# Two layernorm chunks as one background task: norms in two steps of three, scaling at the end

## The chip, the cores and the metric

The kernel runs on one core of one Trainium2 chip. The metric is the device time of one execution in microseconds (us); a kernel is judged by its fast executions (a slow one runs at a granted TensorE clock well below full speed). In the profile's lines PE is TensorE, the matmul engine, PEld its weight loads, DVE is VectorE, ACT ScalarE, POOL GpSimd and SP the engine that issues the transposing DMAs. Beside each time the profile gives the span, from the first to the last instruction; the time is 1.8 us longer than the span.

## The reference

One transformer block, 2048 rows of 1024, with a modulated layernorm ahead of both halves:

```python
h = _layernorm(x) * (1 + ca) + sa
x = x + ga * _A_ref(h, k_cache, v_cache, wq, wo)       # 32 heads over the last 512 keys, output projection
h = _layernorm(x) * (1 + cb) + sb
x = x + gb * _B_ref(h, w_gate, w_up, w_down)           # silu(h @ w_gate) * (h @ w_up) @ w_down, F = 3584
```

## The kernel before

The order is: attention of the first 1024 rows, their output projection, attention of the other 1024, their output projection, gate, up and down projection of the first half, then of the second. Large products are built from seven products of half size instead of eight; each of the seven passes over four row tiles of 128.

While such a projection runs, a background task prepares the layernorm of the next 1024 rows: two chunks of four row tiles. For a tile VectorE writes the normed rows to one of **two** row buffers, and a transposing DMA turns them into `hT`. Once a chunk's four tiles are turned, VectorE scales and shifts it in place. The task advances by one `yield` for each call of `run_bg`.

```python
def norm_turn(ch, tt, tiles, sl=None):
    t = ch * TPC + tt
    sl = t % 2 if sl is None else sl
    norm(t, t % 8, sl, half=True)                       # L438, VectorE, 0.54 us, writes row buffer sl
    T.op(Q_ln[sl], lambda: SP.dma_start_transpose(hT[ch % 2][:, :, tt * P:(tt + 1) * P], nscf[sl]),
         reads=[B_ns4[sl]], writes=[tiles[tt]])         # L465

def ln_task(ch, gi, ccol, cbuf):
    ...
    for tt in range(TPC):                               # TPC = 4
        norm_turn(ch, tt, tiles)
        yield
    for _ in range(3):
        yield
    for dt in range(DT):                                # DT = 8
        modulate(dst, bufs, dt, gi, ccol, cbuf, tiles)  # L443, VectorE, 0.41 us
        if dt % 2 == 1:
            yield
```

The host of the task is `seven_products`. `hook` loads weights and calls `run_bg(1)`; `out` is the residual pass, whose first instruction (L1117) reads the accumulator bank that a later product needs.

```python
for j in range(TPC):
    prod(0, j, AB[j], True, early[j])
    if own_s1:
        s1_sum(j)                                       # L1057, VectorE, 1.23 us
        s2_sum(j)                                       # L1041, VectorE, 1.23 us
    ...
    hook(0, j)                                          # steps 0 to 3; j == 3 first issues the load for product 2
for j in range(TPC):
    prod(1, j, BB_[j], True)
    out(0, j, 0, AB[j], BB_[j], None)                   # residual j frees bank AB[j]
    hook(1, j)                                          # steps 4 to 7
for j in range(TPC):
    prod(2, j, AB[j], False)                            # PE needs AB[j] again
    ...
```

The softmax here doesn't subtract the row's maximum and nothing guards it: scores larger than these inputs give would overflow.

Of the kernel before, what the change touches and what calls it, by code (L numbers as in the profile page):

```python
# [131 lines left out]
def bass_adaLN_cond__sliding_block_cached__swiglu_ffn__prompt_kernel(  # L132
# [14 lines left out]
    _, S, D = A_x.shape  # L147
# [6 lines left out]
    DT = D // P  # L154
# [5 lines left out]
    TPC = CH // P  # L160
# [58 lines left out]
    def bank(b, n=512, off=0):  # L219
        return ps[:, b * 512 + off:b * 512 + off + n]  # L220
# [14 lines left out]
    B_mode = _Buf("mode"); B_modc = _Buf("modc"); B_bq = _Buf("bq"); B_gf = _Buf("gf")  # L235
# [23 lines left out]
    with nc.Block() as block:  # L259

        @block.gpsimd
        def _(g):
# [5 lines left out]
            def mm(out_ap, lhsT, rhs, start, stop, reads, bank_buf, skip=False):  # L268
                T.op(PE, lambda: TE.matmul(out_ap, lhsT, rhs, start=start, stop=stop, skip_group_check=skip),  # L269
                     reads=reads, writes=[bank_buf])  # L270
# [5 lines left out]
            bg = []  # L276

            def run_bg(n=1):
                while n > 0 and bg:
                    try:  # L280
                        next(bg[0])
                        n -= 1
                    except StopIteration:
                        bg.pop(0)
# [88 lines left out]
            B_hT = [[_Buf("hT%d_%d" % (i, dt)) for dt in range(DT)] for i in range(2)]  # L373
            hT = [arena.at(OFF_H + i * 8 * KB, [DT, CH], F16, B_hT[i]) for i in range(2)]
# [61 lines left out]
            def norm(t, sl, ns, c0=0, n=D, half=False):  # L436
                o = (nscf if half else nsc4)[ns]
                T.op(DVE, lambda: V.tensor_scalar(o[:, c0:c0 + n], x_res[:, t, c0:c0 + n], mv[sl][:, 0:1], rstd[sl],  # L438
                                                  op0=ALU.subtract, op1=ALU.mult),
                     reads=[B_x[t], B_mv[sl], B_rs[sl]], writes=[B_ns4[ns]])  # L440

            def modulate(dst, bufs, dt, gi, ccol, cbuf, tiles):
                T.op(DVE, lambda: V.tensor_scalar(dst[:, dt, :], dst[:, dt, :], gain[gi][:, dt:dt + 1],  # L443
                                                  mod_bf[:, ccol + dt:ccol + dt + 1], op0=ALU.mult, op1=ALU.add),
                     reads=[B_g[gi], cbuf] + tiles, writes=[bufs[dt]])
# [8 lines left out]
            def ln_tiles(ch):  # L454
                tiles = [_Buf("hTt%d_%d" % (ch, tt)) for tt in range(TPC)]
                for tile in tiles:
                    for b_ in B_hT[ch % 2]:
                        tile.absorb(b_)
                return tiles
# [4 lines that stand above are left out]
                norm(t, t % 8, sl, half=True)  # L464
                T.op(Q_ln[sl], lambda: SP.dma_start_transpose(hT[ch % 2][:, :, tt * P:(tt + 1) * P], nscf[sl]),  # L465
                     reads=[B_ns4[sl]], writes=[tiles[tt]])

            def ln_task(ch, gi, ccol, cbuf):
                dst, bufs = hT[ch % 2], B_hT[ch % 2]
                tiles = ln_tiles(ch)  # L470
                for tt in range(TPC):
                    norm_turn(ch, tt, tiles)
                    yield
                for _ in range(3):
                    yield
                for dt in range(DT):
                    modulate(dst, bufs, dt, gi, ccol, cbuf, tiles)
                    if dt % 2 == 1:
                        yield

            def stats_task(t0, n):
                for t in range(t0, t0 + n):
                    yield from ln_stats(t)
# [859 lines left out]
            def o_phase(sc, hook):  # L1343
                load, ver = wo0[sc]
                n1 = _N1()
                sj = []

                def rings(tt, j, half):
                    if (tt, half) == (1, 0):
                        return sj[1 + j % 2]  # L1350
                    return tmp[j % 2][:, :], B_tmp[j % 2]

                def hk(idx, j):
                    if j == TPC - 1 and idx < 4:
                        load(idx + 2)
                    if idx == 4 and j == 0:
                        load(6)
                    if j == TPC - 1 and idx == 2:
                        for n in range(TPC):
                            b_ = _Buf("sj%d" % n)  # L1360
                            sj.append((arena.at((128 + 2 * n) * KB, [CH], F32, [b_]), b_))
                    hook(idx, j)

                seven_products(HP, oT, B_oT, OFF_OT, n1, ver, AB_O, BB_O, o_out(sc, sj, rings), sj, True, hk, (14, 14, 0, 0))
# [33 lines left out]

            while bg:
                run_bg(1)  # L1400
            for ch in (2, 3):
                bg.append(ln_task(ch, 0, 0, B_mode))
            o_phase(0, o_hook0)


# [30 lines left out]
            def w_slot(q):  # L1436
                return (q if q < FP else q + 2) % 3

            def take_w(q):
                p = q % FP  # L1440
                sl = w_slot(q)
                W_of[q] = [seven_at(OFF_W[sl] + 8 * KB * m, "w%d_%d" % (q, m), "own") for m in range(2)]
                for m, w in enumerate(W_of[q]):
                    src = (B_w_gate, B_w_up)[m][:, 256 * p:256 * p + 256].rearrange("(k q) n -> q k n", q=P)
                    T.op(Q_w[sl][m], lambda: SP.dma_start(w.raw, src), writes=[w.b_raw, w.b_s3])
# [15 lines left out]
            def ws(n):  # L1461
                for _ in range(n):
                    next(wsum[0], None)
# [18 lines left out]

            while bg:
                run_bg(1)
            for ch in (0, 1):
                bg.append(ln_task(ch, 1, 3 * DT, B_late[1]))
            o_phase(1, o_hook1)
            take_w(1)
            take_w(2)
# [149 lines left out]
            for sc in range(2):  # L1639
                q0 = sc * FP  # L1640

                def f_early(k0, k1):
                    for k in range(k0, k1):
                        va, vb = ver(0, k)
                        mm(bank(0), gu[0][:, k, 0:P], va, k == 0, False, [B_gu[0][k], vb], PB[0], skip=True)

                for r in range(FP + 1):
                    if sc == 0 and r == 2:
                        bg.append(stats_task(2 * TPC, 2 * TPC))
                    gate_up(q0 + r if r < FP else None, q0 + r - 1 if r > 0 else None, f_early if r == FP else None)  # L1650
                    run_bg(3)
                    if 1 <= r < FP - 2:
                        take_w(q0 + r + 2)
                    if r == FP - 2:
                        lq = q0 + FP - 1
                        d0, d1 = OFF_W[w_slot(lq - 2)], OFF_W[w_slot(lq - 1)]
                        load, ver = loader(sc, B_w_down, wd_sum, FP, "d", [[(o, FP)] for o in [d0, d1] * 3 + [d0]])
                        load(0)
                    if r == FP - 1:
                        load(1)  # L1660
                if sc == 0:
                    take_w(FP)
                b_sj = [_Buf("fj%d_%d" % (sc, j)) for j in range(TPC)]
                sj_t = arena.at(OFF_U, [TPC, CH], F32, b_sj)
                sj = [(sj_t[:, j, :], b_sj[j]) for j in range(TPC)]
                if sc == 0:
                    for ch in (2, 3):
                        bg.append(ln_task(ch, 1, 3 * DT, B_late[1]))

                def f_hook(idx, j):  # L1670
                    if j == TPC - 1 and idx < 5:
                        load(idx + 2)
                    run_bg(1)
                    if sc == 0 and idx == 6:
                        if j == 0:
                            while bg:
                                run_bg(1)
                            hs[0] = h_sums()
                            wsum[0] = w_sums(FP)
                        next(hs[0])  # L1680
                        ws(1)

                seven_products(FP, gu, B_gu, OFF_GU, m1, ver, (0, 1, 2, 3), (4, 5, 6, 7), f_out(sc), sj, False, f_hook, (10, 0, 0, 0), sc == 1)
                if sc == 0:
                    take_w(FP + 1)
                    take_w(FP + 2)
                    gu = [arena.at(OFF_GU[n], [FP, CH], F16, B_gu[n]) for n in range(4)]
# [31 lines left out]
```

## Time and profile before

| what | value |
|---|---|
| time, median of the 3 runs known at first | 1151.99 us (1151.91 to 1152.01) |
| span of the profiled execution | 1151.0 us (time of that execution 1152.78) |
| PE busy | 1138.7 us, 99% |
| VectorE (DVE) busy | 822.4 us, 71% |
| VectorE before a norm (L438), waiting for a transposing DMA | 24.8 us, 6 places, longest 7.3 |
| PE standing still behind L1117 | 1.15 us, once, at 570.64 us |

The lines are in the prediction. In a timeline or a chain the first number is the start, counted from the start of the span, the second the length; a bracket at the end gives the engine's idle time just before and what ended it. In a list of waits the numbers are the total, how often, and the longest.

### The profile page before, as it was taken

The page shows a single profiled execution, that of the slowest core. Times are in us where ns is not written, and L with a number is a line of the kernel's source. Part 1 is how long each engine was busy: PE and PEld are TensorE (multiplying, and loading weights), DVE is VectorE, ACT ScalarE, POOL GpSimd, SP SyncE. Part 2 cuts the span into 40 slices and gives each one's busy share as a digit, 9 for nine tenths or more (in the row PEclk, how much of TensorE's full clock was granted, in tenths as well). Part 3 has the DMA queues.
Part 4 walks back from the last instruction along what each step waited for, and adds up shares of the span by engine and source line. Part 5 has one row for each costly group of instructions (what it writes and reads, how often), then busy time and mean ns, then how long its engine had stood idle before and what let it go on. Part 6 is the DMA issues. An engine that isn't in the chain of part 4 may idle for free.

```text
span 1151.0 us, 17926 instructions
## 1 busy us (share of the span) xinstructions
PE 1138.7 (99%) x6906; PEld 584.3 (51%) x6991; DVE 822.4 (71%) x1644; ACT 525.6 (46%) x719; POOL 50.8 (4%) x107
## 2 busy tenths in 40 slices
PE   8999999999999999999999999999999999999999
PEld 5666665554446656656444444444444444444444
DVE  5768779857667777776667789877658777776536
ACT  4757777711137777777010354544110445444110
POOL 1100002100000000001000000000000000000000
PEclk9999999999999999999999999999999999999999
DMA  9889899987717998956784422323773433234343
GB/s 326 142 185 227 224 219 233 198 206 184 214 44 177 212 215 179 213 112 155 144 222 142 111 73 85 98 74 106 209 222 123 119 88 96 74 104 134 128 156 110
DMA packets 300373, 180.83 MB, mean 157 GB/s; under 512 B 140928, under 2 KB 289152, under 8 KB 300288
## 3 DMA queue, kind: packets, MB, share of 16 engines
q1 hardware_dynamic: 241632, 108.90, 41.9%
q10 hardware_dynamic: 54336, 55.05, 15.1%
q0 software_dynamic: 4320, 15.73, 4.7%
q8 instruction: 55, 0.90, 0.3%
q14 instruction: 30, 0.25, 0.1%
HBM read 126.75 MB, written 19.93 MB: 127 GB/s over the span
## 4 chain that ended last, share of the span: by engine, by line
PE 95%; DMA 2%; DVE 1%; issue 1%; ACT 1%; DVEq 0%
PE ps L269 95%; DMA arena<-nsc 1%; ACT arena L800 1%; DMA arena<-arena 0%; DVE st L424 0%; DMA x_res<-in_A_x_dram 0%; DVE arena L1057 0%; DVE nsc L438 0%; PE ps L273 0%; DVE arena L830 0%; DVE arena L847 0%; DVE arena L822 0%; DVE mv L544 0%; DVE arena L901 0%; DVE tmp L1117 0%
## 5 line engine op out<-in xcount | busy, mean ns | idle before, releaser
L269 PE MATMUL ps<-arena 128*128 128x512 f16 (+2 forms) x6693 | 1133.1, 330 | 9.0 <-POOL arena L416 2.0
L269 PEld LDWEIGHTS ps<-arena 128*128 128x128 bf16 (+1 forms) x6778 | 577.0, 98 | 559.3 <-DVE arena L830 4.5
L800 ACT ACTIVATE arena<-ps 128x1024 bf16<-128x1024 f32 x256 | 261.5, 1022 | 47.2 <-PE ps L269 35.4
L833 ACT ACTIVATE tmp<-ps 128x512 f32<-128x512 f32 x167 | 99.7, 597 | 299.8 <-PE ps L269 286.1
L901 DVE TENSOR_TENSOR arena<-arena 128x512 f16<-128x512 bf16 x328 | 133.3, 419 | 3.0
L830 DVE TENSOR_TENSOR arena<-ps,tmp 128x512 bf16<-128x512 f32 (+1 forms) x134 | 91.9, 686 | 52.2 <-PE ps L269 34.7
L833 ACT ACTIVATE nsc<-ps 128x512 f32<-128x512 f32 x84 | 50.1, 597 | 93.3 <-PE ps L269 90.9
L822 DVE TENSOR_TENSOR arena<-ps,rl 128x512 f16<-128x512 f32 x128 | 88.5, 691 | 4.7 <-DVE rl L819 0.2
L830 DVE TENSOR_TENSOR arena<-ps,nsc 128x512 f16<-128x512 f32 x84 | 57.3, 687 | 40.3 <-PE ps L269 30.0
L819 DVE RECIPROCAL rl<-ps 128x4 f32<-128x4 f32 x128 | 23.2, 181 | 74.8 <-PE ps L269 73.6
L1534 ACT ACTIVATE arena<-arena 128x512 f16<-128x512 f16 x84 | 49.8, 624 | 32.8 <-DVE arena L830 32.8
L1041 DVE TENSOR_TENSOR arena<-arena 128x2048 f16<-128x2048 f16 (+3 forms) x56 | 56.0, 1011 | 9.3 <-PE ps L269 8.8
L1117 DVE TENSOR_TENSOR tmp<-ps,tmp 128x512 f32<-128x512 f32 x32 | 22.1, 689 | 55.7 <-ACT tmp L833 46.1
L833 ACT ACTIVATE arena<-ps 128x512 f32<-128x512 f32 x16 | 9.6, 597 | 86.4 <-PE ps L269 86.4
L951 DVE TENSOR_TENSOR arena<-arena 128x512 f16<-128x512 bf16 x120 | 47.9, 420 | 1.0
L424 DVE BATCH_NORM_STATS2 st<-x_res 128x6 f32<-128x512 bf16 x58 | 39.6, 682 | 3.7 <-DMA x_res<-in_A_x_dram 3.4
L602 DVE SCALAR_TENSOR_TENSOR arena<-arena 128x1024 bf16<-128x1024 bf16 x32 | 38.9, 1216 | 0.0
L1549 DVE TENSOR_TENSOR arena<-arena 128x512 f16<-128x512 f16 x84 | 35.0, 417 | 0.3
L1118 DVE TENSOR_TENSOR tmp<-tmp,rowb 128x512 f32<-128x512 f32 (+1 forms) x49 | 33.6, 687 | 1.8
L438 DVE TENSOR_SCALAR nsc<-x_res,mv,rstd 128x1024 f16<-128x1024 bf16 (+1 forms) x30 | 16.2, 539 | 24.8 <-DMA arena<-nsc 24.8
L1119 DVE TENSOR_TENSOR arena<-tmp,x_res 128x512 bf16<-128x512 f32 (+1 forms) x33 | 22.3, 676 | 1.1
L830 DVE TENSOR_TENSOR arena<-ps,rowb 128x512 f16<-128x512 f32 x28 | 19.3, 689 | 3.8 <-ACT rowb L833 3.3
(80 smaller groups left out, 295.5 us busy)
## 6 DMA issues: line engine op xcount, KB each, us to landing
arena<-in_A_wq_dram SPq DMA_DIRECT2D x30, 512.0 KB, 5.2
arena<-wo_sum ACTq DMA_DIRECT2D x7, 2048.0 KB, 8.7
arena<-in_B_w_gate_dram SPq DMA_DIRECT2D x28, 512.0 KB, 3.9
arena<-in_B_w_up_dram SPq DMA_DIRECT2D x28, 512.0 KB, 5.1
arena<-wd_sum ACTq DMA_DIRECT2D x8, 1792.0 KB, 8.0
arena<-in_B_w_down_dram ACTq DMA_DIRECT2D x6, 1792.0 KB, 7.1
arena<-in_A_wo_dram POOLq DMA_DIRECT2D x16, 512.0 KB, 5.6
wo_sum<-arena SPq DMA_DIRECT2D x16, 512.0 KB, 4.0
```

What stands on the lines that cost most here:

```text
L269: T.op(PE, lambda: TE.matmul(out_ap, lhsT, rhs, start=start, stop=stop, skip_group_check=skip), reads=reads, writes=[bank_buf])
L424: T.op(DVE, lambda: V.bn_stats(st_[sl][:, hf * 6:hf * 6 + 6], x_res[:, t, hf * 512:hf * 512 + 512]), reads=[B_x[t]], writes=[B_st[sl]])
L602: T.op(DVE, lambda: V.scalar_tensor_tensor(mt[n % 2], mt[n % 2], 1.0, sc_row, op0=ALU.mult, op1=ALU.mult, accum_out=mcol[:, n:n + 1]), rea ...
L800: T.op(ACT, lambda: A.activation(ex_s[es][:, 2 * kp:2 * kp + 2, :], banks2(SCB + 2 * kp), AF.Exp, scale=att_scale), writes=[PB[SCB + 2 * k ...
L822: T.op(DVE, lambda: V.tensor_tensor(o_s[os_].rearrange("p (a b) d -> p a b d", a=2), psap(PVB * 512, [[512, 2], [130, 2], [1, P]]), rlb, A ...
L830: T.op(DVE, lambda: V.tensor_tensor(out, bank(ba), other, ADD), reads=[ob2], writes=[PB[ba], ob])
L833: T.op(ACT, lambda: A.activation(dst, bank(bk), AF.Copy), writes=[PB[bk], db])
L901: T.op(st, lambda: eng.tensor_tensor(o, a, b, op), reads=rd, writes=[wr])
L951: T.op(DVE, lambda: V.tensor_tensor(o, a, b, SUB), reads=rd, writes=[wr])
L1041: T.op(DVE, lambda: V.tensor_tensor(o, a, b, SUB), reads=rd, writes=[sb])
L1534: T.op(ACT, lambda: A.activation(o, s_, AF.Silu), reads=[sb], writes=[ob])
L1549: T.op(DVE, lambda: V.tensor_tensor(gu[blk][:, p, :], o, s_, MULT), reads=[sb, ob], writes=[B_gu[blk][p]])
```

## The change

The aim is that a norm no longer meets a row buffer that is still being transposed. The two chunks become one task; norms come in two steps of three; both chunks are scaled at the end.

```diff
-            def ln_task(ch, gi, ccol, cbuf):
-                dst, bufs = hT[ch % 2], B_hT[ch % 2]
-                tiles = ln_tiles(ch)
-                for tt in range(TPC):
-                    norm_turn(ch, tt, tiles)
+            def ln_pair(chs, gi, ccol, cbuf):
+                tiles = {ch: ln_tiles(ch) for ch in chs}
+                for n in range(2 * TPC):
+                    norm_turn(chs[n // TPC], n % TPC, tiles[chs[n // TPC]])
                     yield
-                for _ in range(3):
-                    yield
-                for dt in range(DT):
-                    modulate(dst, bufs, dt, gi, ccol, cbuf, tiles)
-                    if dt % 2 == 1:
+                    if n % 2 == 1:
                         yield
+                for ch in chs:
+                    for dt in range(DT):
+                        modulate(hT[ch % 2], B_hT[ch % 2], dt, gi, ccol, cbuf, tiles[ch])
+                        if dt % 2 == 1:
+                            yield
...
-            for ch in (0, 1):
-                bg.append(ln_task(ch, 1, 3 * DT, B_late[1]))
+            bg.append(ln_pair((0, 1), 1, 3 * DT, B_late[1]))
```

The same replacement is made in the first output projection and in the down projection.

More of the change, by code (lines that the diff above doesn't have):

```diff
@@ L1400, in _ @@
                 run_bg(1)
-            for ch in (2, 3):
-                bg.append(ln_task(ch, 0, 0, B_mode))
+            bg.append(ln_pair((2, 3), 0, 0, B_mode))
             o_phase(0, o_hook0)
@@ L1666, in _ @@
                 if sc == 0:
-                    for ch in (2, 3):
-                        bg.append(ln_task(ch, 1, 3 * DT, B_late[1]))
+                    bg.append(ln_pair((2, 3), 1, 3 * DT, B_late[1]))
                 def f_hook(idx, j):
```

## The prediction

> **What bounds the kernel now.** I read the page first, for the share of each engine; then the list of waits kept to the tensor engine; then the chain that ended last; then the timeline of the three stretches that the change touches, engine by engine.
>
> ```profile
> PE 1138.7 (99%) x6906; PEld 584.3 (51%) x6991; DVE 822.4 (71%) x1644; ACT 525.6 (46%) x719; POOL 50.8 (4%) x107
> ...
> DVE nsc L438 <- DMA arena<-nsc: 24.8, 6, 7.3
> ...
> PE ps L269 <- POOL arena L416: 2.0, 1, 2.0
> PE ps L269 <- DVE tmp L1117: 1.2, 1, 1.2
> PE ps L269 <- DVE arena L516: 0.5, 1, 0.5
> PE ps L269 <- DVE arena L830: 0.4, 2, 0.2
> PE ps L269 <- ACT arena L800: 0.3, 1, 0.3
> ```
>
> The first line says that PE is busy for 1138.7 of 1151.0 us: all that any change of order can give back is the 12.3 us in which it stands still. The second is the wait that the change is aimed at: VectorE stands for 24.8 us, in six places, before a norm of the layernorm (L438) because the row buffer that the norm writes is still being read by the transposing DMA of two tiles before. The last five are PE's own waits by releaser. Only one of them lies in a layernorm stretch and comes from VectorE's output code: 1.2 us, once, behind L1117, the first addition of a residual. So 24.8 us of VectorE's waiting show up as 1.2 us of PE's. The chain that ended last shows how the two hang together, in the output projection of the second half of the rows:
>
> ```profile
> 547.36 5.53 DMA arena<-arena
> 553.01 1.24 DVE arena L1057
> 554.31 1.10 issue
> 555.42 0.54 DVE nsc L438
> 555.99 10.50 DMA arena<-nsc
> 566.58 0.10 DVE nsc L438
> 566.68 0.36 issue
> 567.04 1.23 DVE arena L1057
> 568.33 1.11 issue
> 569.44 0.54 DVE nsc L438
> 569.98 0.61 DVE tmp L1117
> 570.64 27.80 PE ps L269 x128
> ```
>
> Columns are start, length, what. The chain leaves PE at 546 us, goes through VectorE and two transposing DMAs, and comes back to PE only at 570.64. The timeline of PE there has the gap itself (start, length, engine):
>
> ```profile
> 540.74 28.74 PE L269 MATMUL ps<-arena 128*128 128x512 bf16 x152
> 570.64 79.61 PE L269 MATMUL ps<-arena 128*128 128x512 f16 x366 [1.15 <-DVE tmp L1117]
> ```
>
> 540.74 + 28.74 = 569.48, then nothing until 570.64. What PE waits for at 570.64 is an accumulator bank: the third of the seven products adds into the banks of the first, and the first residual pass (L1117) has to read such a bank before PE may write it again.
>
> **What the Trainium skill says.** "Perfetto Trace Analysis", section "Optimization Strategy", says to find the gaps on the engine being optimised and what blocks it there. That is the reading used above; it leaves one gap in these stretches, not the 24.8 us. "PSUM — Partial Sum Buffer", section "Engine vs sequencer instructions": "ScalarE/VectorE/GpSimdE queues are strict FIFO." The trace agrees: the two sums of the fourth row tile, whose data were there when PE ended the first product at about 555.3, ran at 567.04 and 568.30, behind a norm that waited until 566.58. "DMA: Bandwidth & Descriptors", section "Issuing engines are not separate DMA queues", says that DMAs from different issuers end up on the same 16 engines and interleave. The trace agrees: the transposes issued at 555.99 and 558.84 from SP took 10.5 and 8.4 us, since ACT had issued a 2 MB load at 555.27 that landed at 564.64; the next two, with no load under way, took 3.06 us each. "TensorE: Matmul & The Clock Gate", section "Back-to-back issue gap", gives N/2.4 + 2.5 ns for an isolated matmul, 216 ns for N = 512; here ScalarE's evictions of successive products come 3.45 us apart (559.16, 562.62), 216 ns for each of the 16 matmuls, so PE is at its pace.
>
> **The change part by part.** I call one call of the hook after a row tile's product a step: 16 matmuls, 3.45 us, in the two output projections; 14, 3.02 us, in the down projection. Steps 0 to 3 belong to the first product, 4 to 7 to the second, and so on. Each step runs one piece of the background task, after that step's own VectorE work.
>
> Removed and added: no arithmetic. There are 8 norms at 0.54 us, 8 transposes and 16 scalings at 0.41 us per stretch in both. The old task has 22 steps: norms of chunk a in 0 to 3, empty 4 to 6, scaling in 7 to 10, norms of chunk b in 11 to 14, empty 15 to 17, scaling in 18 to 21. The new one has 20: norms in 0, 1, 3, 4, 6, 7, 9, 10, empty between, scaling of a in 12 to 15, of b in 16 to 19. Both end before step 23, where the sums over the transposed rows start, so no consumer comes forward. The direct saving of instructions is 0.
>
> Moved, in the stretch with the gap. Old order on VectorE: sums 0, norm 0, sums 1, norm 1, sums 2, norm 2 (waits until 566.58), sums 3, norm 3, residual. The residual can begin at 566.58 + 0.46 (norm issue) + 2.40 (two sums of 1.23, pipelined) + 0.46 (norm) = 569.90, which is what the timeline shows, and its bank is free at 569.90 + 0.68 = 570.58. New order: sums 0, norm 0, sums 1, norm 1, sums 2, sums 3, norm 2, residual 0, norm 3. Up to norm 1 (558.73) it is unchanged. Sums 2 and 3 take 4 x 1.23 and end by 563.7. Norm 2 waits for the same DMA, landed at 566.48, so it starts at 566.58 as before. The residual then starts at 566.58 + 0.46 = 567.04, 2.86 us earlier, and frees its bank at 567.72. PE arrives there at 569.48. So the whole 1.15 us goes, with 1.76 us to spare; the other 1.7 us of VectorE's gain are nothing to PE. The other three banks have a step more each: residual 1 is read by about 570.4 (after norm 3, whose buffer landed at 567.26), against 572.9 on PE.
>
> The other two stretches. In the first output projection PE's last matmul of the second product ends at about 261.4 (evictions at 251.04 and 254.49, then every 3.45) and the bank was free at 259.84 + 0.68 = 260.52: no wait before, so no gain, though VectorE's residual also comes 2.86 us earlier. In the down projection norms 0 to 3 never waited: 0 to gain. Elsewhere code and order are the same.
>
> Sum: -1.15 us, 1151.99 - 1.15 = 1150.84. VectorE's own wait at L438 I expect to fall to about 12 us (8 to 18), not to nothing: norm 2 still waits in the second projection (2.9 us when sums 3 end at 563.7) and the norm in step 9 meets the transpose of step 6, which now leaves just as a load of 2 MB is issued; some 3 us in each of the three stretches (estimate, from the 8 to 9 us that such transposes took and two and a half steps of distance).
>
> **The rivals.** (1) *The whole 24.8 us come back.* Then about 1127, 2.2% faster. For it speaks only the size of the wait; against it, PE is still for 12.3 us in all, and most of that is at the start of the kernel. (2) *Nothing moves: the wait changes its place.* Norm 2 and the transpose of tile 0 are on the path in both kernels; if that transpose landed 1.8 us later than in this trace, or norm 3 came to wait before residual 1, PE would stand again. Then 1151 to 1152. For it: transposes beside a load differ by 2 us (8.4 to 10.5). (3) *A new wait.* The norms of steps 9 and 10 stand behind a load, and the in-order queue holds the subtractions of steps 9 to 11 with them. Their products come in step 16, over 13 us later, against a stop of some 3 to 8 us. Hidden, unless two such stops add up. (4) *VectorE fills up in the down projection.* Steps 16 to 19 now carry a residual (0.72 + 0.73 + 0.61) and a pair of scalings (0.65), 2.7 us of 3.02. The old kernel did the same in steps 18 to 21 without a PE wait. If it slips, under 1 us. (3) and (4) would give 1151.5 to 1155.
>
> **Range and chances.** The three timed runs lie within 0.1 us, the profiled one is 0.8 above them. I take 1150.8, with the rest of rivals 2 and 3 on the upper side and the spread between chips around it: 1150.0 to 1152.2. Two per cent are 23 us; a gain of that size would be twice what PE has idle, and a loss of that size would need a stop that no buffer here can make. So 0.01 faster, 0.98 within 2%, 0.01 slower.
>
> **What would show it right or wrong.** In the new profile: PE's list of waits has no entry behind L1117, and the rest is unchanged; PE's busy time is 1138.7 give or take 0.5, and the span shorter by about 1.1; in the second output projection residual 0 starts 2.8 us or so before the gap's old end and PE runs through; VectorE's wait at L438 is 8 to 18 us; the chain no longer passes a transpose of the layernorm there. A PE wait behind L1117, L1041 or L443 in any of the three stretches, or a span changed by more than 2 us, would make the prediction wrong.

## The result

The changed kernel took 1152.57 us (median of 6 runs, 1151.79 to 1153.60), the kernel before 1152.26 us (6 runs, 1151.91 to 1153.65). The ratio is 1.000, with a 95% interval of 0.9988 to 1.0013. Ratios here are the mean time of one kernel's fast runs over that of the other's of the same rounds, so not quite the ratio of the medians quoted. There is no change; the prediction said 1150.8 and a range up to 1152.2, and the measured median lies above it.

Most of the profile looks like the prediction. First the page's busy line of the changed kernel, its wait at the norms, and PE's own waits:

```profile
PE 1144.0 (99%) x6991; PEld 584.4 (51%) x6991; DVE 822.4 (71%) x1644; ACT 526.0 (46%) x719; POOL 51.3 (4%) x107
```

```profile
DVE nsc L438 <- DMA arena<-nsc: 11.9, 4, 4.3
...
PE ps L269 <- POOL arena L416: 2.0, 1, 2.0
PE ps L269 <- DVE arena L830: 0.8, 2, 0.5
PE ps L269 <- DVE arena L516: 0.6, 1, 0.6
```

VectorE's wait at the norms halved, from 24.8 to 11.9 us, and L1117 is gone from PE's list. PE's busy time rose from 1138.7 to 1144.0 because the trace of before lacks records: it has 6906 matmuls, this one 6991 (the later profiles of before, b_p2 to b_p4, lack as many and give 1139.0 to 1139.4). In the timeline of PE the second output projection is now inside one unbroken stretch, and in that of VectorE norm 2 follows the sums of tile 3 without any wait and the first residual follows it:

```profile
499.68 648.15 PE L269 MATMUL ps<-arena 128*128 128x512 f16 x3189
```

```profile
560.40 1.22 DVE L1057 TENSOR_TENSOR arena<-arena 128x2048 f16<-128x2048 f16 x1
561.65 1.23 DVE L1041 TENSOR_TENSOR arena<-arena 128x2048 f16<-128x2048 f16 x1
562.79 0.54 DVE L438 TENSOR_SCALAR nsc<-x_res,mv,rstd 128x1024 f16<-128x1024 bf16 x1
563.25 0.68 DVE L1117 TENSOR_TENSOR tmp<-ps,tmp 128x512 f32<-128x512 f32 x1
```

Yet the span is shorter by 0.3 us only (1150.95 against 1150.62), and the median time not at all. To see why, cut the span at one landmark: the end of the last exponential of attention (L800). Call what lies before it the **head**, what lies after it the **tail**, where PE had stopped. Before: head 544.16, tail 606.79. After: head 545.15, tail 605.47. So the tail lost 1.32 us, of which 1.15 is the stop itself, and the head was 0.99 us longer.

The head is not free of the change: it holds the first output projection, where the same edit is made. A second cut, at the end of the last exponential of the first half's attention, settles what the edit costs there. From this cut to the end of the head it is 308.12 us in both kernels, and 308.12 or 308.13 in every profile at full clock, whatever the order; so the edit costs nothing there. The 0.99 us lie before the cut (236.04 against 237.03), where both kernels have the same code. That left two questions: is the head's difference, which lies in unchanged code, chance, and is the stop in the tail there in each execution of the kernel before?

### The profile page after: what moved, and what is told of

Same layout as the page of the kernel before. It is cut to its first block, busy times and chain, and to the rows that moved or that the text cites. A ratio compares the mean times of both kernels' runs of the same rounds, so it can differ in the third digit from the quotient of the medians.

```text
span 1150.6 us, 18014 instructions
## 1 busy us (share of the span) xinstructions
PE 1144.0 (99%) x6991; PEld 584.4 (51%) x6991; DVE 822.4 (71%) x1644; ACT 526.0 (46%) x719; POOL 51.3 (4%) x107
## 4 chain that ended last, share of the span: by engine, by line
PE 97%; SPq 1%; DMA 1%; DVE 0%; ACT 0%; issue 0%; DVEq 0%
PE ps L269 97%; DMA arena<-in_w_mod_dram 1%; SPq L337 0%; SPq L360 0%; ACT arena L800 0%; DVE arena L830 0%; SPq L306 0%; SPq L355 0%; DVE arena L847 0%; SPq L378 0%; SPq L396 0%; DVE arena L901 0%; DVE tmp L1112 0%; DVE arena L1119 0%; DVEq L80 0%
## 5 line engine op out<-in xcount | busy, mean ns | idle before, releaser
L800 ACT ACTIVATE arena<-ps 128x1024 bf16<-128x1024 f32 x256 | 261.7, 1022 | 47.4 <-PE ps L269 35.7
L830 DVE TENSOR_TENSOR arena<-ps,tmp 128x512 bf16<-128x512 f32 (+1 forms) x134 | 91.9, 686 | 52.1 <-PE ps L269 34.7
L830 DVE TENSOR_TENSOR arena<-ps,nsc 128x512 f16<-128x512 f32 x84 | 57.3, 687 | 40.3 <-PE ps L269 30.0
L1117 DVE TENSOR_TENSOR tmp<-ps,tmp 128x512 f32<-128x512 f32 x32 | 22.1, 690 | 64.4 <-ACT tmp L833 61.7
L438 DVE TENSOR_SCALAR nsc<-x_res,mv,rstd 128x1024 f16<-128x1024 bf16 (+1 forms) x30 | 16.1, 538 | 12.0 <-DMA arena<-nsc 11.9
L830 DVE TENSOR_TENSOR arena<-ps,rowb 128x512 f16<-128x512 f32 x28 | 19.3, 689 | 3.8 <-ACT rowb L833 3.3
```

The costliest lines, as they stand in the source:

```text
L800: T.op(ACT, lambda: A.activation(ex_s[es][:, 2 * kp:2 * kp + 2, :], banks2(SCB + 2 * kp), AF.Exp, scale=att_scale), writes=[PB[SCB + 2 * k ...
L830: T.op(DVE, lambda: V.tensor_tensor(out, bank(ba), other, ADD), reads=[ob2], writes=[PB[ba], ob])
```

## The experiments

The theories. **A**: every execution of before has the stop, the change removes it, and the head's scatter hides the gain. **B**: the stop is a race between the first tile's transpose and a 2 MB weight load, lost in some executions only. **C**: the change costs elsewhere what it gains. A slip runs through the first expectations: they give the length of the tail as 406.8 and 405.5 us; it is 606.8 and 605.5, the subtraction was 200 too low. The differences are not touched by it.

### Both kernels again: b_again, a_again

No edit.

> The kernel before, byte for byte, as a null test and a second profile of it. Theory A (the stop of PE behind L1117 in the second output projection is there in every execution; the scatter of the start hides its removal): the profile shows a stop of PE there of 1.0 to 1.4 us; ratio 1.000 within 0.0005. Theory B (the stop is a race between the first tile's transpose and the 2 MB load, there in some executions only): the stop may be anywhere from 0 to 1.4 us, and it goes with how long the first transpose takes (8 us or more: stop; under 5 us: none). Theory C (the change costs elsewhere what it gains) says nothing here. All: single times scatter over more than 1 us, and the moment at which PE enters the second output projection scatters as much.

> The changed kernel, byte for byte. Theory A: ratio to before 0.9990 (1.15 of 1152 us) with an interval of about 0.0006, no stop of PE behind L1117 in the profile. Theory B: ratio between 0.9990 and 1.0000. Theory C: ratio 1.0000 or over, and some landmark after the second output projection lies later against its start than in the kernel before. The stretch from PE's start of the second output projection to the end of the kernel is shorter than in a run of before by 1.0 to 1.4 us under A, by nothing or up to 1.4 under B, by nothing under C.

b_again: 1152.91 us median of 5 runs, the slow one among them (1152.60 for the four fast ones); its profiled execution is slow (1720.46 us at a granted clock of 0.655) and is used for nothing. Its fast runs against the shared runs of before: ratio 1.0001 (0.9987 to 1.0014). a_again: 1152.50 us, ratio 1.0002 (0.9989 to 1.0014). The 0.9990 of theory A is at the edge of the second interval. Its tail is 605.46 us, as in the first profile of this kernel, and no stop lies behind L1117: C, a cost elsewhere, has no place, in the tail by this length and in the head by the 308.12 us above.

### The old order with four row buffers: b_rows4

Two more row buffers, for the second output projection alone, in memory that held keys and is dead by then. No norm of the first chunk can wait for a transpose.

```diff
+            b4 = [_Buf("xr0"), _Buf("xr1")]
+            four["rows"] = [(nscf[n], B_ns[n]) for n in range(2)] + [(arena.at(OFF_KT + 2 * n * KB, [D], F16, [b4[n]]), b4[n]) for n in range(2)]
...
-                    norm_turn(ch, tt, tiles)
+                    (norm_turn4 if four else norm_turn)(ch, tt, tiles)
```

> The kernel before in its old order, but with four row buffers instead of two for the norms of the second output projection (two more in memory that is dead by then), so that no norm of the first chunk waits for a transpose. If the stop of PE comes from that wait (A and B), PE does not stop there, the residual starts about 563.7 us on the scale of the first profile, and the time equals that of the changed kernel within noise (A: ratio 0.9990; B: as the changed kernel). If the stop comes from VectorE's amount of work, it stays and the ratio is 1.000.

1152.20 us, ratio 0.9998 (0.9984 to 1.0011). The stop is not there and the tail is 605.46 us. But this profiled execution took 1154.58 us, because its head was 547.28 us. PE's timeline shows where part of that went, in the attention of the first half, where both kernels have the same code (L842 is L830 of the kernel before, moved by the edit):

```profile
190.31 9.80 PE L269 MATMUL ps<-arena 128*128 128x512 f16 x80 [1.40 <-DVE arena L842]
200.26 949.69 PE L269 MATMUL ps<-arena 128*128 128x512 f16 x5314 [0.15 <-DVE arena L842]
```

A stop of 1.40 us in attention, which no other profile has, is as large as all that the change could give.

### Joined but not spread: a_nopace

The pair as one task, a norm in every step.

```diff
                     yield
-                    if n % 2 == 1:
-                        yield
+                for _ in range(4):
+                    yield
```

> The pair as one task, each chunk scaled once both are turned, but a norm in every step (8 norms in steps 0 to 7, then four empty steps): the second half of the change alone. A and B: the first four norms stand where they stood before, so the stop of PE behind L1117 is that of the kernel before (1.0 to 1.4 us where the first transpose is late) and norms of the second chunk add waits of VectorE ahead of residuals in steps 4 to 7, which may lengthen it by up to 3 us: ratio 1.000 to 1.003. If it was the joining that helped, the stop is gone and the ratio is as the changed kernel's.

1152.92 us, ratio 1.0006 (0.9994 to 1.0019); tail 605.46 us, no stop. The first four norms stand where they stood before the change, so by A the stop should have been here. VectorE's timeline shows why it was not:

```profile
561.02 0.54 DVE L438 TENSOR_SCALAR nsc<-x_res,mv,rstd 128x1024 f16<-128x1024 bf16 x1
...
566.59 0.55 DVE L438 TENSOR_SCALAR nsc<-x_res,mv,rstd 128x1024 f16<-128x1024 bf16 x1 [2.64 <-DMA arena<-nsc]
567.05 0.68 DVE L1117 TENSOR_TENSOR tmp<-ps,tmp 128x512 f32<-128x512 f32 x1
```

Norm 2, at 561.02, waited for nothing: transpose 0 had been issued 0.88 us *before* the load and took 3.36 us. Norm 3 waited, with only the residual behind it. A falls here, as far as the first four norms decide the stop; the next profiles, of the old kernel itself, settle it. B stands.

### The kernel before, three more profiles: b_p2, b_p3, b_p4

No edit.

> The kernel before once more, byte for byte, for a profile in the fast state. If the stop of PE behind L1117 is there in every execution: 1.0 to 1.4 us, and 406.5 to 407.0 us from the end of attention (the last exponential) to the end of the span, as in the first profile (406.8). If it is a race: the stop goes with the time of the first tile's transpose; under 6 us no stop and 405.4 to 405.6 us, as the four profiles without a stop have.

> The kernel before, byte for byte, a further profile for the share of executions with a stop. Race theory: transpose 0 issued over 0.5 us after the load: it takes 9 us or more, stop of 0.5 us or more and 606 us or over from the end of attention; issued earlier: no stop and 605.5.

> The kernel before, byte for byte, as b_p3: transpose 0 over 0.5 us behind the load goes with a stop of 0.5 us or more and 606 us or over from the end of attention; issued earlier, no stop and 605.5 us.

Times 1151.85, 1152.83 and 1152.16 us. **None of the three has the stop**; the tails are 605.46, 605.47 and 605.47. In b_p2, VectorE at the place of the stop, and PE:

```profile
564.06 0.55 DVE L438 TENSOR_SCALAR nsc<-x_res,mv,rstd 128x1024 f16<-128x1024 bf16 x1 [3.08 <-DMA arena<-nsc]
...
567.28 0.55 DVE L438 TENSOR_SCALAR nsc<-x_res,mv,rstd 128x1024 f16<-128x1024 bf16 x1 [0.28 <-DMA arena<-nsc]
567.74 0.68 DVE L1117 TENSOR_TENSOR tmp<-ps,tmp 128x512 f32<-128x512 f32 x1
```

```profile
231.06 916.20 PE L269 MATMUL ps<-arena 128*128 128x512 bf16 x4991 [0.31 <-ACT arena L800]
```

Norm 2 still waits 3.08 us, but the residual starts at 567.74, 23.15 us after the end of attention, and PE comes for its bank 25.32 us after it (569.48 - 544.16 in the first profile). VectorE's wait is there in this execution too; PE does not feel it.

### The load held back: b_hold

The old order; ScalarE, which issues the load, first waits for transpose 0.

```diff
...
+                    if sc == 1 and j == TPC - 1 and idx == 0:
+                        t0 = _Buf("t0")
+                        t0.last_write = (Q_ln[0], ln0[0])
+                        T.op(ACT, lambda: A.activation(acc[:, 0:1], mhalf[:, 0:1], AF.Copy), reads=[t0, B_mh], writes=[B_acc])
                     if j == TPC - 1 and idx < 4:
                         load(idx + 2)
...
```

> The kernel before in its old order, with the 2 MB load of the third product held until the first tile's transpose has landed, so that the race always goes well. Race theory: transpose 0 takes under 5 us, no stop behind L1117, 405.4 to 405.7 us from the end of attention to the end of the span, and ratio 1.000 (0.9990 if the plain kernel nearly always stops). The load then lands at about 568, 1 us before PE needs it; if it is later, a stop of PE for that load of under 1 us takes the place. If the stop comes from VectorE's work and not from the transposes, it stays at 1.0 to 1.4 us.

1152.44 us, ratio 1.0000 (0.9987 to 1.0012). Transpose 0 took 3.08 us, the first residual ended at 20.36 us after attention, no stop, tail 605.47; the load, issued 3.18 us after the transpose, landed 24.54 us after attention, in time for PE. The race won on purpose changes nothing, as the plain kernel mostly wins it by itself.

### Two attempts to lose the race that did not: b_forced, a_forced, b_late, a_late

The first pair adds a 0.5 MB load as the first sums end; the second adds one unused VectorE addition of 1.22 us ahead of norm 0. Each is made in the old and the new order.

```diff
...
+                    T.op(Q_extra, lambda: A.dma_start(xt, A_wo[0:4 * P, 0:512].rearrange("(k p) n -> p k n", p=P)),
+                         reads=[sum0], writes=[spare])                  # b_forced, a_forced
...
+                    T.op(DVE, lambda: V.tensor_tensor(spare, x_res[:, 0:2, :], x_res[:, 2:4, :], ADD),
+                         reads=B_x[0:4], writes=[b_sp])                 # b_late, a_late
```

> The kernel before with one more load of 0.5 MB into dead memory, issued as the first sums of the second output projection end, so that the first tile's transpose is behind a load in every execution. Race theory: transpose 0 takes 9 us or more each time, norm 2 waits for it, PE stops 1 to 3 us behind L1117; ratio to before 1.001 to 1.002 if the plain kernel mostly has no stop, 1.000 to 1.001 if it always has one.

> The changed kernel with the same extra load. If the change is worth anything where the transpose is late, it shows here: no stop of PE or one of under 0.5 us, 1 to 2.5 us less than b_forced in the profile from the end of attention to the end of the span, and ratio to before of 1.000. If the change is worth nothing even then, it equals b_forced.

> The kernel before with one addition of 128x2048 (1.22 us of VectorE, result unused) ahead of norm 0 of the second output projection, so that transpose 0 is issued 0.5 to 2 us after the 2 MB load instead of 1.0 us before to 0.7 us after it. Race theory, from the profiles so far: behind the load the transpose lands some 22.3 us after the end of attention, the residual ends at some 26.4, PE comes for the bank at 25.3: a stop of 0.9 to 1.6 us, now in every execution, 606.4 to 607.1 us from the end of attention to the end of the span against 605.5 without a stop (the earlier expectations gave these lengths as 406.8 and 405.5: 200 too low by a slip). Times about 1 us above a_late's. Rival (the addition only delays and the load does not matter): the residual ends 1.2 us later than in the runs without a stop, at 21 to 25, and there is no stop.

> The changed kernel with the same addition. Race theory: transpose 0 is as late as in b_late (22.3 us after the end of attention), norm 2 waits for it, but the residual follows it at once and ends at some 23.6, before PE comes at 25.3: no stop, 605.5 us from the end of attention to the end. Times 1 us below b_late's, equal to the plain kernels' within noise. Rival: as b_late.

Ratios: b_forced 1.0009 (0.9996 to 1.0023), a_forced 0.9997 (0.9985 to 1.0010), b_late 1.0000 (0.9987 to 1.0013), a_late 0.9998 (0.9984 to 1.0011). No profile of the four has the stop; all tails are 605.46 or 605.47. The expectations missed. In b_late transpose 0 was issued 0.63 us behind the load, as late as in the first profile (0.71), but landed 20.46 us after attention instead of 22.32. The two timelines of VectorE, b_late then a_late, show how the new order uses the same landing better, to no profit for PE:

```profile
565.04 0.55 DVE L438 TENSOR_SCALAR nsc<-x_res,mv,rstd 128x1024 f16<-128x1024 bf16 x1 [3.60 <-DMA arena<-nsc]
...
568.35 0.68 DVE L1117 TENSOR_TENSOR tmp<-ps,tmp 128x512 f32<-128x512 f32 x1
```

```profile
565.05 0.55 DVE L438 TENSOR_SCALAR nsc<-x_res,mv,rstd 128x1024 f16<-128x1024 bf16 x1 [1.04 <-DMA arena<-nsc]
565.51 0.69 DVE L1117 TENSOR_TENSOR tmp<-ps,tmp 128x512 f32<-128x512 f32 x1
```

From the wait's end to the residual's start it is 3.31 us in the old order, 0.46 in the new: the 2.85 us that the prediction had worked out as 2.86. In b_late PE came 0.77 us after the bank was free.

### A push meant to lose the race each time: b_push, a_push

Three unused additions (2.1 us together) ahead of norm 0, and a further 0.75 MB load right behind the 2 MB one, in both orders.

```diff
+                    for _ in range(3):
+                        T.op(DVE, lambda: V.tensor_tensor(spare, x_res[:, 0, :], x_res[:, 1, :], ADD), ...)
...
                         load(idx + 2)
+                    if sc == 1 and j == TPC - 1 and idx == 0:
+                        T.op(dq("q_extra", nc.scalar), lambda: A.dma_start(
+                            xt, A_wo[0:6 * P, 0:512].rearrange("(k p) n -> p k n", p=P)), writes=[more])
```

> The kernel before with two additions in the second output projection: three unused sums of 128x1024 (1.8 us in all) ahead of norm 0, so that transpose 0 comes 0.8 to 2.5 us behind the 2 MB load, and a further load of 0.75 MB right behind that load. Race theory: transpose 0 now lands 23.5 to 25 us after the end of attention instead of 13 to 22, the first residual ends 4.1 us after that, at 27.6 to 29, against PE's coming at 25.3: a stop of 2.3 to 3.7 us behind L1117 in every execution, 607.8 to 609.2 us from the end of attention to the end of the span, ratio 1.002 to 1.003. Rival (transposes do not matter to PE, what the one profile showed was an accident of something else): no stop, 605.5.

> The changed kernel with the same two additions. Race theory: norm 2 waits for the same late transpose, the residual ends 1.2 us after it instead of 4.1, at 24.7 to 26.2: a stop of 0 to 0.9 us, 605.5 to 606.4 us from the end of attention to the end, 1.5 to 3 us less than b_push in the profile and in the mean of the timed runs. Rival one: equal to b_push with a stop (the order does not matter). Rival two: both without a stop.

b_push: 1157.45 us (median of 6, 1154.18 to 1159.06), ratio 1.0040 (1.0027 to 1.0053). a_push: 1152.61 us (median of 5, 1152.29 to 1152.66), ratio 1.0003 (0.9991 to 1.0015). The means are 1156.89 and 1152.50: **4.4 us between the two orders**. Only one execution of each was profiled; but all six times of b_push lie above all eleven of the plain kernel in the same rounds (1151.15 to 1153.05). PE and VectorE in b_push:

```profile
231.81 338.85 PE L269 MATMUL ps<-arena 128*128 128x512 bf16 x2317 [0.31 <-ACT arena L800]
573.69 579.22 PE L269 MATMUL ps<-arena 128*128 128x512 f16 x2674 [3.03 <-DVE tmp L1117]
```

```profile
569.64 0.55 DVE L438 TENSOR_SCALAR nsc<-x_res,mv,rstd 128x1024 f16<-128x1024 bf16 x1 [6.08 <-DMA arena<-nsc]
...
572.95 0.68 DVE L1117 TENSOR_TENSOR tmp<-ps,tmp 128x512 f32<-128x512 f32 x1
```

and in a_push:

```profile
568.22 0.55 DVE L438 TENSOR_SCALAR nsc<-x_res,mv,rstd 128x1024 f16<-128x1024 bf16 x1 [3.11 <-DMA arena<-nsc]
568.68 0.69 DVE L1117 TENSOR_TENSOR tmp<-ps,tmp 128x512 f32<-128x512 f32 x1
```

```profile
231.86 916.20 PE L269 MATMUL ps<-arena 128*128 128x512 bf16 x4991 [0.31 <-ACT arena L800]
```

So the mechanism of the prediction is real and the new order does remove the stop. (Part of the pair's difference is scatter: transpose 0 landed 24.20 us after attention in b_push, 22.73 in a_push. With 22.73 the old order would end the residual at about 26.8, still 1.5 us too late; with 24.20 the new one at about 25.4, on the edge.) The tail of b_push is 610.36, 4.89 over the undisturbed 605.47, but the stop is 3.03. The rest is in the view by windows, whose columns are the window, its length, PE busy and how many matmuls, the same for the other engines, then the granted clock, the busy share of the DMA engines and GB/s:

```profile
570.60:573.60 3.00, 0.06 (x1) 0.00 (x0) 2.97 (x4) 0.00 (x0) 0.00 (x0) 1.00 0.45 87
573.69:577.20 3.51, 3.51 (x10) 1.32 (x11) 3.41 (x6) 0.60 (x1) 0.00 (x0) 0.56 0.39 75
577.20:580.60 3.40, 3.40 (x17) 1.47 (x16) 3.26 (x6) 0.60 (x1) 0.00 (x0) 0.95 0.66 204
```

After the stop PE ran 10 matmuls in 3.5 us where 16 fit at full speed (216 ns each): the clock was granted at half for 3.413 us (the trace's clock record, from 574.12). Half of that, 1.71 us, is lost on top: 3.03 + 1.71 = 4.74 of the 4.89. The expectation had the stop right (2.3 to 3.7 us) and missed the rest by this clock: it had a tail of 607.8 to 609.2, a ratio of 1.002 to 1.003 and 1.5 to 3 us between the two orders.

### All profiles side by side

Times in us, without the slow profile of b_again; the residual's end and the landing are counted from the end of attention; on that count PE comes for the bank at 25.32.

| profile | order | head | transpose 0 issued against the load | took | landed | residual 0 ends | stop of PE | tail |
|---|---|---|---|---|---|---|---|---|
| before | old | 544.16 | +0.71 | 10.50 | 22.32 | 26.41 | 1.15 | 606.79 |
| b_p2 | old | 544.59 | +0.07 | 8.20 | 19.38 | 23.84 | 0 | 605.46 |
| b_p3 | old | 545.52 | -0.03 | 8.17 | 19.25 | 23.83 | 0 | 605.47 |
| b_p4 | old | 544.88 | -0.13 | 5.61 | 16.59 | 23.93 | 0 | 605.47 |
| b_forced | old | 545.01 | -0.14 | 6.22 | 17.19 | 24.34 | 0 | 605.46 |
| b_late | old | 544.49 | +0.63 | 8.72 | 20.46 | 24.55 | 0 | 605.47 |
| b_rows4 | old, four row buffers | 547.28 | -0.22 | 5.62 | 16.51 | 20.01 | 0 | 605.46 |
| b_hold | old | 545.16 | -3.18 | 3.08 | 13.73 | 20.36 | 0 | 605.47 |
| b_push | old | 545.34 | +1.88 | 11.21 | 24.20 | 28.30 | 3.03 | 610.36 |
| a_nopace | old in the first four norms | 545.66 | -0.88 | 3.36 | 13.59 | 22.08 | 0 | 605.46 |
| after | new | 545.15 | -0.99 | 3.35 | 13.46 | 18.78 | 0 | 605.47 |
| a_again | new | 545.17 | -0.46 | 5.95 | 16.61 | 19.32 | 0 | 605.46 |
| a_forced | new | 544.67 | -0.38 | 6.26 | 17.00 | 19.40 | 0 | 605.46 |
| a_late | new | 544.62 | +0.67 | 8.56 | 20.34 | 21.58 | 0 | 605.47 |
| a_push | new | 545.39 | +1.00 | 10.63 | 22.73 | 23.98 | 0 | 605.47 |

In the old order the residual ends 4.1 us after transpose 0 lands, if nothing else is later; so PE stops when that landing is past about 21.2 us. Of the four profiles of the plain kernel before at full clock, one has it there (the three later ones are single runs, so their state is on record as unknown; their granted clock is 1.0). Where PE does not stop, the tail is 605.46 or 605.47 in every kernel: the tail hardly scatters at all. The head scatters over 3 us (544.16 to 547.28, with b_rows4), and all of it arises before the end of the first half's attention (236.04 to 239.15), in code that the change doesn't touch.

## Why the prediction was wrong

**What bounds the kernel** was right: PE bounds it, and VectorE's 24.8 us of waiting meant next to nothing. The "12.3 us in which it stands still" was too high, as the trace lacked matmul records; the list of PE's waits in the same profile sums to under 5 us. The prediction cites the Trainium skill, "TensorE: Matmul & The Clock Gate", section "Back-to-back issue gap", for the 216 ns of an isolated matmul. It leaves out that the same section gives about 131 ns each for a sustained stream at N = 512. Here the stream itself ran at 216 ns (16 matmuls in 3.45 us): that this is the pace of PE rests on the trace, not on the page.

**The mechanism** was right: one bank, behind one residual, behind one norm, behind one transpose. The order worked out as 2.86 us faster measured 2.85 (b_late against a_late), the wait at the norms fell to 11.9 us where "about 12" was said, PE met none of the new waits that the rivals named, and b_push against a_push shows the stop and its removal. The 11.9 is right in part by luck: the norm of step 9 waited 2.83, 2.87 and 4.34 us in the three stretches, as foretold ("some 3 us" each), but norm 2 of the second projection, given 2.9, did not wait, as transpose 0 came early; norm 3 waited 1.88 instead.

**The step that failed** is "Sum: -1.15 us, 1151.99 - 1.15 = 1150.84". It subtracts a stop seen in one profiled execution from the median of three others. The 1.15 us was to be multiplied by the share of executions that have it: one of four profiles. All 11 fast runs of the changed kernel in the two sets of rounds that timed it (mean 1152.59, spread 0.49 as a standard deviation) and the 51 runs of before in all sets (48 fast, and the three single ones at full clock; mean 1152.47, spread 0.67) differ by +0.12 with a standard error of about 0.18. By this a gain of more than about 0.24 us in the mean is unlikely (two standard errors), while a gain of 1.32 us in one execution of four would be 0.33: the share is probably smaller than four profiles suggest (an estimate). The data were there: the profiled execution had taken 1152.78, 0.8 over the timed three. Their spans were then about 1150.2 by the 1.8 us difference, and with the stop's tail of 606.79 their heads would have been 543.4, shorter than any head measured. So the three timed runs probably had no stop; that is argued, not shown.

**The range** failed by the same step. The prediction read three runs within 0.1 us as the scatter, and centred the range on them. They lay 0.5 us under the mean of the 51. Of the 1.75 us between the 1150.84 of the prediction and the mean of 1152.59, 0.48 are that base, and 1.27 the gain that isn't in the mean.

**Rival 2** came nearest: it said that the landing of transpose 0 decides and that its time by a load varies, and gave 1151 to 1152, still under the measured 1152.57. It looked for that scatter in the changed kernel only, not in the kernel before.

What stays open: why transpose 0, issued 0.7 us behind the load both times, landed at 22.32 in one profile and at 20.46 in another; and what makes the head scatter, of which the profiles show only the place. Nor is it known whether the share of executions with the stop differs between chips: the later profiles came from several, and the chip of the first is not on record. No experiment here tells these.

## What to carry to other kernels

A stop seen in one trace is a fact of one execution: before its length is subtracted from a median, look at two or three more traces, and ask whether a race of two transfers set it. Cut the span at landmarks and compare piece by piece, those that the change touches and those that it cannot; that showed 1.3 us here where whole times, with a spread of 0.7 us, showed nothing. A change that only widens a margin can still be right: it made no mean faster here, but when the transfers were made late, the new order lost nothing that shows and the old one 4.4 us, some of it by the scatter of the landing.

## What the Trainium skill lacked or had wrong

- "TensorE: Matmul & The Clock Gate", section "What's actually happening", has the clock halved after at least one idle window of about 3.4 us. Here a stop of 3.03 us was enough, in the one profile that has such a stop (the page's closing table, "Why this matters for your kernels", says gaps over about 3 us, which fits). The clock fell at 574.12, 0.43 us after PE had resumed, and was at half for 3.413 us, the length that the section gives for the window; by estimate that costs another 1.71 us. The stop of 1.15 us cost no clock (1.00 in the windows after it).
- "DMA: Bandwidth & Descriptors", section "Issuing engines are not separate DMA queues", says that transfers of different issuers interleave, not how much the order of issue matters: the same transpose took 3.1 to 3.4 us when issued 0.9 us or more before a 2 MB load, 5.6 to 6.3 when 0.1 to 0.5 before, 8.2 when level with it, 8.6 to 10.5 when 0.6 to 0.7 behind.
- "Perfetto Trace Analysis", section "Optimization Strategy", has the reader look for gaps in a trace; it doesn't say that a gap can be there in one execution and not in the next. This one was in 1 of 4 profiles of the same kernel.
- Neither the page on TensorE nor the one on traces says that matmul records can be missing: 6906 of 6991 were there in the first trace, and the busy time of PE was 5.3 us lower than in a full one.
